# Turning the keys with VectorE in 32x32 blocks of 32-bit words, in a cached-attention decode kernel

## The chip, the cores and the metric

The kernel runs on one core of one Trainium2 chip. The metric is the time of the whole program in microseconds of device time, as a median of several runs. The traces are of one profiled execution each; a trace's span (first to last instruction) is about 2 us shorter than the run's time. In this kernel TensorE does the matrix products, VectorE and ScalarE the copies, reductions and exponentials, and GpSimd next to nothing (0.9 us busy before). HBM is the memory that the inputs are read from; the loads bring them to tiles in SBUF, and the profile takes their share over 16 DMA engines. The kernel keeps the products of TensorE in PSUM; to copy them from there to SBUF is to *evict* them. In the profiles PE is TensorE, PEld its loading of weights, DVE VectorE, ACT ScalarE and POOL GpSimd. The *granted clock* is the share of TensorE's full clock that it was given.

A single-core run shows no second die to compare with, so its "slow" label means only that the run is over 1.5% above the fastest run of the same kernel.

## The reference, cut to what matters

```python
# B=8 sequences, one new token each; Hq=16 query heads, Hkv=8 key/value heads, Dh=256, window W=1024
q = (x @ wq) -> [B, 16, 1, 256]
k, v = caches[:, :, Sk-W:, :]  (each head serves 2 query heads)
p = softmax(q @ k.T * Dh**-0.5);  a = (p @ v) @ wo
b = layernorm -> MLP(448 -> 1792 -> 448)
out = g * a + (1 - g) * b          # g: a sigmoid gate per token
```

The bytes are the keys and the values: 64 (sequence, head) pairs of 1024 x 256 bf16 each, keys and values 67 MB together, and 10.6 MB of weights. All are read once.

## The kernel before: the parts that matter

The work is cut into 16 *units* of four key/value heads. A unit has 2 MiB of keys (one tile in SBUF, partition = 32 positions x 4 heads) and 2 MiB of values. A ring of nine 2 MiB slots feeds everything: a load is issued as soon as a slot is released.

```python
RING = 9; LAG = 3                                # values of unit u are used LAG units later
def transpose_keys(u, between):                  # TensorE turns, ScalarE and VectorE evict
    for hf in range(2):
        for i in range(4):
            for c in range(8):
                nc.tensor.transpose(ktp[:, c, :], kn[:, o : o + P], ident[:])   # 128x128
            (nc.scalar.copy or nc.vector.tensor_copy)(kt[...], ktp[:])
            for step in between.get(g, ()): step()     # softmax of unit u-1 goes in between
    done()                                       # releases the slot of the keys

def scores(u):                                   # four heads side by side: 16 products of 628 ns in 2.01 us
    for hf in range(2):
        for j in range(2):
            for a in range(4):
                nc.tensor.matmul(S_ps[32*a : 32*a + 8, ...], lhsT=qw[:, j, b, half, a, :],
                                 rhs=KT[hf][:, j, :, a::4], ...)
...
for u in range(1, 16):
    transpose_keys(u, steps(u - 1))
    if u >= LAG: values(u - LAG)
    scores(u); top(u)
    if u >= LAG: finish(u - LAG)
```

## Time and profile before

| | before |
|---|---|
| time, median of 4 runs | 194.23 us (194.14 to 194.64) |
| span of the traced run | 192.3 us |
| HBM read | 77.68 MB |
| DMA, 50 to 170 us | share 1.01 of 16 engines, 425 GB/s |
| TensorE / VectorE / ScalarE busy | 78% / 63% / 44% |
| granted TensorE clock, mean | 0.910 |

The page of the profile. In the line of an engine, the figures are busy us, share of the span and number of instructions. The rows of digits are 40 slices of the span in tenths (9 is 90% or more). The last lines are groups of instructions: what was written and read, the count, then busy us and mean ns, then the idle time of that engine before them.

```profile
span 192.3 us, 4534 instructions
...
PE 150.7 (78%) x1990; PEld 104.7 (54%) x1990; DVE 121.5 (63%) x278; ACT 83.9 (44%) x102; POOL 0.9 (0%) x7
...
PEclk9998597899999999999999958999999999985558
DMA  5999999999999999999999999999999999999970
...
L342 ACT COPY kt<-ktp 128x1024 bf16<-128x1024 bf16 x64 | 63.2, 1017 | 70.8 <-PE ktp L339 70.8
L339 PE MATMUL ktp<-ident,slot 128*128 128x128 bf16 x1024 | 72.8, 229 | 19.3 <-ACT kt L342 10.4
...
L344 DVE COPY kt<-ktp 128x1024 bf16<-128x1024 bf16 x64 | 41.3, 684 | 15.0 <-PE ktp L339 15.0
L385 PE MATMUL S_ps<-kt,qw 128*8 128x512 bf16 x256 | 32.4, 628 | 0.3 <-DVE qw L375 0.3
```

The DMA row is full from the second slice to the last but two. What the change removes, the key transposes and their copies, is the largest work on three engines, but it runs under a full DMA. The chain of waits (start us, us, what), its end:

```profile
90.11 40.68 DMA slot<-in_A_k_cache_dram
130.85 39.20 DMA slot<-in_A_v_cache_dram
170.07 18.62 DMA slot<-in_A_wo_dram
```

From 90 us on the chain is nothing but loads. A unit's 4.19 MB take 9.8 to 9.9 us at 425 to 428 GB/s; that is the pace that any version must keep.

One more reading matters later: the granted clock of TensorE, by stretches (us; busy us of each engine; then clock, DMA share, GB/s).

```profile
50.00:170.00 120.00, 101.18 (x1306) 68.90 (x1304) 88.73 (x181) 62.79 (x78) 0.00 (x0) 0.97 1.01 425
...
109.50:110.50 1.00, 0.00 (x0) 0.00 (x0) 0.10 (x1) 0.00 (x0) 0.00 (x0) 0.70 1.07 442
110.50:111.50 1.00, 0.34 (x4) 0.35 (x5) 0.00 (x0) 0.00 (x0) 0.00 (x0) 0.50 1.00 426
```

TensorE is busy 84% of this time and its clock is 0.97 of full; once, while it waits for keys from 108.6 to 111.2 us, the clock falls to 0.50.

### The profile page before, as it was taken

The page shows a single profiled execution, that of the slowest core. Times are in us where ns is not written, and L with a number is a line of the kernel's source. Part 1 is how long each engine was busy: PE and PEld are TensorE (multiplying, and loading weights), DVE is VectorE, ACT ScalarE, POOL GpSimd, SP SyncE. Part 2 cuts the span into 40 slices and gives each one's busy share as a digit, 9 for nine tenths or more (in the row PEclk, how much of TensorE's full clock was granted, in tenths as well). Part 3 has the DMA queues.
Part 4 walks back from the last instruction along what each step waited for, and adds up shares of the span by engine and source line. Part 5 has one row for each costly group of instructions (what it writes and reads, how often), then busy time and mean ns, then how long its engine had stood idle before and what let it go on. Part 6 is the DMA issues. An engine that isn't in the chain of part 4 may idle for free.

```text
span 192.3 us, 4534 instructions
## 1 busy us (share of the span) xinstructions
PE 150.7 (78%) x1990; PEld 104.7 (54%) x1990; DVE 121.5 (63%) x278; ACT 83.9 (44%) x102; POOL 0.9 (0%) x7
## 2 busy tenths in 40 slices
PE   1199976999898988979888589896969697837672
PEld 0199624855756656575646286745554646413371
DVE  7632313767978787787958547776767676773310
ACT  2343020865848466382818154636354545520000
POOL 1000000000000000000000000000000000000000
PEclk9998597899999999999999958999999999985558
DMA  5999999999999999999999999999999999999970
GB/s 192 418 437 407 431 427 426 424 433 426 419 423 423 423 430 430 426 424 419 426 419 433 421 426 430 423 426 426 423 426 426 426 430 426 430 412 417 417 298 22
DMA packets 6742, 77.97 MB, mean 406 GB/s; under 512 B 946, under 2 KB 1347, under 8 KB 1987
## 3 DMA queue, kind: packets, MB, share of 16 engines
q1 hardware_dynamic: 6512, 77.67, 96.0%
q8 instruction: 15, 0.25, 0.5%
q10 hardware_dynamic: 210, 0.02, 0.1%
q14 instruction: 5, 0.03, 0.0%
HBM read 77.68 MB, written 0.01 MB: 404 GB/s over the span
## 4 chain that ended last, share of the span: by engine, by line
DMA 51%; PE 29%; ACT 12%; DVE 5%; issue 1%; ACTq 0%; DVEq 0%; SPq 0%
DMA slot<-in_A_k_cache_dram 21%; DMA slot<-in_A_v_cache_dram 20%; DMA slot<-in_A_wo_dram 10%; PE ktp L339 9%; PE S_ps L385 8%; ACT kt L342 7%; ACT E L405 4%; PE PO L446 3%; PE S_ps L356 2%; PE hT L494 2%; PE hT L484 1%; PE sm L471 1%; PE bb L532 1%; DVE nmx L397 1%; PE sm L424 1%
## 5 line engine op out<-in xcount | busy, mean ns | idle before, releaser
L342 ACT COPY kt<-ktp 128x1024 bf16<-128x1024 bf16 x64 | 63.2, 1017 | 70.8 <-PE ktp L339 70.8
L339 PE MATMUL ktp<-ident,slot 128*128 128x128 bf16 x1024 | 72.8, 229 | 19.3 <-ACT kt L342 10.4
L339 PEld LDWEIGHTS <-slot 128*128 128x128 bf16 x1024 | 67.1, 105 | 25.9 <-issue 15.5
L344 DVE COPY kt<-ktp 128x1024 bf16<-128x1024 bf16 x64 | 41.3, 684 | 15.0 <-PE ktp L339 15.0
L385 PE MATMUL S_ps<-kt,qw 128*8 128x512 bf16 x256 | 32.4, 628 | 0.3 <-DVE qw L375 0.3
L397 DVE TENSOR_REDUCE nmx<-S_ps 128x1 f32<-128x1024 f32 x16 | 19.6, 1225 | 15.0 <-PE S_ps L385 15.0
L413 DVE STREAM_TRANSPOSE EB<-E 128x1024 bf16<-128x1024 bf16 x16 | 19.9, 1245 | 7.0 <-ACT E L405 6.7
L405 ACT ACTIVATE E<-S_ps,nmx 128x1024 bf16<-128x1024 f32 x16 | 17.9, 1120 | 3.3 <-DVE nmx L398 3.3
L446 PE MATMUL PO<-slot,ET 128*16 128x512 bf16 x256 | 18.4, 410 | 1.2 <-DMA slot<-in_A_v_cache_dram 1.2
L385 PEld LDWEIGHTS <-qw 128*8 128x8 bf16 x256 | 7.3, 94 | 14.8 <-issue 10.4
L446 PEld LDWEIGHTS <-ET 128*16 128x16 bf16 x256 | 5.4, 91 | 6.8 <-issue 2.2
L426 DVE CAST ET<-sm 128x256 bf16<-128x256 f32 x16 | 6.6, 414 | 0.7 <-PE sm L424 0.7
L474 DVE CAST oT<-sm 128x16 bf16<-128x16 f32 x16 | 3.5, 220 | 3.3 <-PE sm L471 3.3
L424 PE MATMUL sm<-selr,ones_f 128*128 128x8 f32 x32 | 5.3, 239 | 0.0
L424 PEld LDWEIGHTS sm<-selr,ones_f 128*128 128x128 f32 x32 | 5.0, 196 | 0.5 <-issue 0.4
L421 PE MATMUL sm<-EB,perm 128*128 128x256 bf16 x16 | 4.5, 279 | 0.3 <-DVE oT L474 0.3
L594 PE MATMUL A_ps<-slot,oP 128*8 128x112 bf16 x128 | 3.8, 287 | 0.8 <-DMA slot<-in_A_wo_dram 0.8
L504 DVE TENSOR_TENSOR z<-hT,b_sb 128x112 f32<-128x112 f32 x1 | 0.3, 275 | 5.5 <-PE hT L494 5.5
L594 PEld LDWEIGHTS <-oP 128*8 128x8 bf16 x128 | 2.9, 116 | 1.6 <-issue 1.6
L356 PE MATMUL S_ps<-slot,xT 128*8 128x512 bf16 x32 | 3.4, 607 | 0.0
L229 PE MATMUL tp<-ident,y_sb 8*128 8x8 bf16 x3 | 0.2, 170 | 3.8 <-DVE y_sb L280 3.8
L405 ACT ACTIVATION_READ_ACCUMULATOR E<-S_ps,nmx 128x1 f32 x16 | 3.2, 202 | 0.0
(143 smaller groups left out, 86.8 us busy)
## 6 DMA issues: line engine op xcount, KB each, us to landing
slot<-in_A_v_cache_dram SPq DMA_DIRECT2D x16, 2048.0 KB, 37.5
slot<-in_A_k_cache_dram SPq DMA_DIRECT2D x15, 2048.0 KB, 34.5
slot<-in_A_wo_dram SPq DMA_DIRECT2D x3, 896.0 KB, 31.0
slot<-in_A_k_cache_dram SPq DMA_DIRECT2D x2, 1024.0 KB, 7.1
slot<-in_A_wq_dram SPq DMA_DIRECT2D x1, 2048.0 KB
slot<-in_B_w_dram SPq DMA_DIRECT2D x1, 1568.0 KB
slot<-in_B_w_dram SPq DMA_DIRECT2D x1, 1344.0 KB, 9.7
slot<-in_A_wq_dram SPq DMA_DIRECT2D x1, 1024.0 KB
```

The costliest lines, as they stand in the source:

```text
L339: nc.tensor.transpose(ktp[:, c, :], kn[:, o : o + P], ident[:])
L342: nc.scalar.copy(dst, ktp[:])
L344: nc.vector.tensor_copy(dst, ktp[:])
L356: nc.tensor.matmul(S_ps[32 * t : 32 * t + NB, n * QN : (n + 1) * QN], lhsT=xT[:, r + half, :], rhs=w[:, o + c : o + c + QN], start=(r == 0 ...
L385: nc.tensor.matmul(S_ps[32 * a : 32 * a + RQ, hf * CH * SK : (hf + 1) * CH * SK], lhsT=qw[:, j, b, half, a, :], rhs=KT[hf][:, j, :, a::QUA ...
L397: nc.vector.reduce_max(nmx[:], S_ps[:], axis=AXIS.X, negate=True)
L405: nc.scalar.activation(E[:], S_ps[:], ACT.Exp, bias=nmx[:], scale=1.0, accum_out=rowsum[:])
L413: nc.vector.transpose(EB[:].rearrange("p c r -> p (c r)"), E[:])
L424: nc.tensor.matmul(sm[:, NCK, :], lhsT=ones_f[:], rhs=selr[:], start=True, stop=True)
L426: nc.vector.tensor_copy(ET[:], sm[:, 0:NCK, :])
L446: nc.tensor.matmul(PO[32 * t : 32 * t + PAIR * RQ], lhsT=ET[:, PAIR * c : PAIR * (c + 1), :], rhs=vn[:, PAIR * c * Dh : PAIR * (c + 1) * D ...
L594: nc.tensor.matmul(dst, lhsT=oP[:, j, q, :], rhs=w[:, o + cols.start : o + cols.stop], start=(q == 0 and j == 0), stop=(q == NHQ - 1 and j ...
```

## The change

The intent: take the 1024 key transposes from TensorE and their 128 evictions from ScalarE and VectorE. VectorE instead turns 32x32 blocks of 32-bit words straight from SBUF to SBUF (two bf16 go as one word). This leaves the keys of the four heads mixed in blocks on the partitions, so the scores use *block-diagonal* queries: full-width products of 128 columns, eight per half unit, plus one that puts a large negative number where the head is foreign. The maximum of a row group is then shared among blocks by a small fp32 product (`share`). LAG goes from 3 to 2, and scores get two PSUM buffers.

```diff
-    LAG = 3
+    LAG = 2
...
-                        nc.tensor.transpose(ktp[:, c, :], kn[:, o : o + P], ident[:])
-                    dst = kt[:, j, c0 : c0 + NC, :]
-                    if g in (0, 3, 4, 7):
-                        nc.scalar.copy(dst, ktp[:])
-                    else:
-                        nc.vector.tensor_copy(dst, ktp[:])
+        nc.vector.transpose(
+            KT[u, hf][:, c0 : c0 + PIECE].rearrange("p c k x r -> p (c k x r)").bitcast(WORD),
+            kn[:, o : o + PIECE * Dh].bitcast(WORD),
+        )
...
+        nc.tensor.matmul(S[u][:, cols], lhsT=foreign[:], rhs=place[:], start=True, stop=False)
+        for k in range(NK):                      # 4
+            for par in range(NPAR):              # 2
+                nc.tensor.matmul(S[u][:, cols], lhsT=qw[:, j, u, m * RQ : m * RQ + P],
+                                 rhs=kt[:, :, k, :, par], start=False, stop=...)
...
+    def share(u):
+        nc.tensor.matmul(mz[:], lhsT=same[:], rhs=m4[:], start=True, stop=True)
+        nc.vector.reduce_max(nmx[:], mz[:], axis=AXIS.X, negate=True)
+        nc.scalar.activation(E, S, ACT.Exp, bias=nmx[:], ...)
...
     for u in range(1, NQ):
-        transpose_keys(u, steps(u - 1))
-        if u >= LAG:
-            values(u - LAG)
-        scores(u)
-        top(u)
+        for piece in range(CH // PIECE):
+            turn_keys(u, 0, piece)
+        scores(u, 0)
+        top(u - 1)
+        turn_keys(u, 1, 0)
+        share(u - 1)
+        turn_keys(u, 1, 1)
+        if u >= LAG:
+            values(u - LAG)
+        scores(u, 1)
+        turn(u - 1)
+        if u >= LAG:
+            gather(u - LAG)
+        invert(u - 1)
         if u >= LAG:
             finish(u - LAG)
```

More of the change, by code (lines that the diff above doesn't have):

```diff
@@ L13 @@
 F32 = mybir.dt.float32
+WORD = mybir.dt.int32
 PSUM = bass.MemoryType.PSUM
@@ L64 @@
     CH = NCK // NH
+    NU = NQ
     SLOT = 8192
@@ L70 @@
     RING = 9
-    LAG = 3
+    LAG = 2
+    NK = 4
+    NPAR = 2
+    KP = NK * NPAR
+    BLK = 32
+    PIECE = 8
     BIG = 1e30
@@ L80 @@
     ring = ctx.enter_context(tc.tile_pool(name="ring", bufs=RING))
-    ktpool = ctx.enter_context(tc.tile_pool(name="ktpool", bufs=4))
+    ktpool = ctx.enter_context(tc.tile_pool(name="ktpool", bufs=3))
     epool = ctx.enter_context(tc.tile_pool(name="epool", bufs=2))
     opool = ctx.enter_context(tc.tile_pool(name="opool", bufs=LAG + 1))
-    ps_s = ctx.enter_context(tc.tile_pool(name="ps_s", bufs=1, space=PSUM))
-    ps_kt = ctx.enter_context(tc.tile_pool(name="ps_kt", bufs=3, space=PSUM))
-    ps_sm = ctx.enter_context(tc.tile_pool(name="ps_sm", bufs=1, space=PSUM))
+    ps_s = ctx.enter_context(tc.tile_pool(name="ps_s", bufs=2, space=PSUM))
+    ps_sm = ctx.enter_context(tc.tile_pool(name="ps_sm", bufs=2, space=PSUM))
     ps_po = ctx.enter_context(tc.tile_pool(name="ps_po", bufs=1, space=PSUM))
@@ L191 @@
     nc.gpsimd.memset(ones_f[:], 1.0)
-    S_ps = ps_s.tile([P, W], F32)
-    nc.vector.memset(S_ps[:], 0.0)
+    Sq = ps_s.tile([P, W], F32, tag="S", name="Sq")
+    nc.vector.memset(Sq[:], 0.0)
     PO = ps_po.tile([P, PAIR, Dh], F32)
@@ L214 @@
     own = consts.tile([P, PAIR], F32)
-    qw = consts.tile([P, NJ, NB, Hq // RQ, QUAD, RQ], BF16)
+    AREA = P + BLK
+    qw = consts.tile([P, NJ, NU, AREA], BF16)
+    pick = consts.tile([P, NK // NJ, NPAR, P], BF16)
+    same = consts.tile([P, P], F32)
+    block = consts.tile([P, QUAD], F32)
+    foreign = consts.tile([P, P], BF16)
+    place = consts.tile([P, CH, BLK], BF16)
     oT = consts.tile([P, Hq, NJ, NB], BF16)
@@ L236 @@
     transposed(xT, x_sb, xz)
+    by_col = ident[:].rearrange("p (b r) -> p b r", b=QUAD)
+    by_row = ident[:].rearrange("p (b r) -> p r b", b=QUAD)
+    nc.vector.reduce_sum(sel[:], by_row[:, 0:RQ, :], axis=AXIS.X)
+    nc.vector.reduce_sum(block[:], by_col, axis=AXIS.X)
+    zrow = consts.tile([P, BLK], F32)
+    nc.vector.reduce_sum(zrow[:], by_row, axis=AXIS.X)
+    nc.vector.tensor_copy(
+        same[:].rearrange("p (b r) -> p b r", b=QUAD),
+        zrow[:].rearrange("p (o r) -> p o r", o=1).to_broadcast([P, QUAD, BLK]),
+    )
@@ L237 @@
+    pairs = zrow[:, 0 : PAIR * RQ].rearrange("p (q i) -> p q i", i=PAIR)
+    nc.vector.reduce_sum(sel2[:], pairs, axis=AXIS.X)
+    nc.vector.reduce_sum(own[:], pairs.rearrange("p q i -> p i q"), axis=AXIS.X)
+    head = consts.tile([BLK, QUAD], F32)
     nc.vector.reduce_sum(
-        sel[:], ident[:].rearrange("p (a s) -> p s a", a=QUAD)[:, 0:RQ, :], axis=AXIS.X
-    )
-    halfs = ident[:].rearrange("p (a s) -> p s a", a=QUAD)
-    for i in range(PAIR):
-        nc.vector.reduce_sum(
-            own[:, i : i + 1], halfs[:, i * RQ : (i + 1) * RQ, :], axis=AXIS.XY
-        )
@@ L245 @@
-    nc.vector.reduce_sum(
-        sel2[:],
-        ident[:]
-        .rearrange("p (a h s) -> p s a h", a=QUAD, s=RQ)[:, :, :, 0:PAIR],
-        axis=AXIS.XY,
-    )
-    perm = consts.tile([P, P], BF16)
-    nc.vector.tensor_copy(
-        perm[:].rearrange("p (s a) -> p s a", a=QUAD),
-        ident[:].rearrange("p (a s) -> p s a", a=QUAD),
-    )
-    cap = consts.tile([P, 1], F32)
-    rows = consts.tile([P, 1], F32)
-    for a in range(QUAD):
-        nc.vector.reduce_sum(
-            rows[32 * a : 32 * a + 32, :],
-            ident[32 * a : 32 * a + 32, (32 + rep) * a : (32 + rep) * a + rep],
-            axis=AXIS.X,
-        )
@@ L264 @@
-    nc.vector.tensor_scalar(
-        cap[:], rows[:], 2.0 * BIG, -BIG, op0=ALU.mult, op1=ALU.add
-    )
+        head[:],
+        ident[0:BLK, 0:BLK].rearrange("p (s a) -> p a s", a=QUAD),
+        axis=AXIS.X,
+    )
+    nc.vector.tensor_scalar(
+        head[:], head[:], BIG, -BIG, op0=ALU.mult, op1=ALU.add
+    )
+    nc.vector.memset(foreign[:], 0.0)
+    for i in range(rep):
+        nc.vector.tensor_copy(
+            foreign[0:BLK, :].rearrange("p (b r) -> p b r", b=QUAD)[:, :, i:RQ:rep],
+            head[:].rearrange("p (o a) -> p o a", o=1).to_broadcast([BLK, QUAD, QUAD]),
+        )
@@ new lines @@
+    nc.vector.tensor_copy(
+        place[:],
+        ident[:, 0:BLK].rearrange("p (o x) -> p o x", o=1).to_broadcast([P, CH, BLK]),
+    )
+    for kk in range(NK // NJ):
+        for par in range(NPAR):
+            nc.vector.tensor_copy(
+                pick[:, kk, par, :].rearrange("p (b w) -> p b w", b=QUAD),
+                ident[:]
+                .rearrange("p (k o w r) -> p k r o w", k=NK // NJ, o=1, r=NPAR)[:, kk, par]
+                .to_broadcast([P, QUAD, BLK]),
+            )
@@ L326, with turn_keys @@
     KT = {}
-    def transpose_keys(u, between=None):
+    def turn_keys(u, hf, piece):
         kn = slot("k", u)
-        between = between or {}
-        for hf in range(NH):
-            kt = ktpool.tile([P, NJ, CH, P], BF16, tag="kt", name="kt")
-            KT[hf] = kt
-            for i in range(CH // NC * NJ):
-                    c0, j = i // NJ * NC, i % NJ
-                    g = hf * (CH // NC * NJ) + i
-                    ktp = ps_kt.tile([P, NC, P], BF16, tag="ktp", name="ktp")
-                    for c in range(NC):
-                        o = (hf * CH + c0 + c) * Dh + j * P
-                        nc.tensor.transpose(ktp[:, c, :], kn[:, o : o + P], ident[:])
-                    dst = kt[:, j, c0 : c0 + NC, :]
-                    if g in (0, 3, 4, 7):
-                        nc.scalar.copy(dst, ktp[:])
-                    else:
-                        nc.vector.tensor_copy(dst, ktp[:])
-                    for step in between.get(g, ()):
-                        step()
-        done()
+        if piece == 0:
+            KT[u, hf] = ktpool.tile(
+                [P, CH, NK, BLK, NPAR], BF16, tag="kt", name="kt"
+            )
+        c0 = piece * PIECE
+        o = (hf * CH + c0) * Dh
+        nc.vector.transpose(
+            KT[u, hf][:, c0 : c0 + PIECE]
+            .rearrange("p c k x r -> p (c k x r)")
+            .bitcast(WORD),
+            kn[:, o : o + PIECE * Dh].bitcast(WORD),
+        )
+        if (hf + 1) * CH == NCK and c0 + PIECE == CH:
+            done()
     def query():
@@ L356, in query @@
                     nc.tensor.matmul(
-                        S_ps[32 * t : 32 * t + NB, n * QN : (n + 1) * QN],
+                        Sq[32 * t : 32 * t + NB, n * QN : (n + 1) * QN],
                         lhsT=xT[:, r + half, :],
@@ L364, in query @@
         done(2)
-        qs = consts.tile([P, W], BF16)
-        nc.scalar.activation(qs[:], S_ps[:], ACT.Copy, scale=qscale)
-        qt = ps_kt.tile([P, NC, P], BF16, tag="ktp", name="qt")
-        for m in range(NC):
-            nc.tensor.transpose(qt[:, m, :], qs[:, m * P : (m + 1) * P], ident[:])
-        qv = qt[:].rearrange(
-            "p (c i j) (g d s) -> p d c j s g i", c=2, i=rep, j=NJ, g=Hq // RQ, d=2
-        )
-        for a in range(QUAD):
-            for j in range(NJ):
-                nc.vector.tensor_copy(
-                    qw[:, j, :, :, a, a * rep : (a + 1) * rep],
-                    qv[:, a // 2, a % 2, j, 0:NB],
-                )
@@ L380, in scores @@
-    def scores(u):
-        b, half = divmod(u, Hkv // QUAD)
-        for hf in range(NH):
-            for j in range(NJ):
-                for a in range(QUAD):
-                    nc.tensor.matmul(
-                        S_ps[32 * a : 32 * a + RQ, hf * CH * SK : (hf + 1) * CH * SK],
-                        lhsT=qw[:, j, b, half, a, :],
-                        rhs=KT[hf][:, j, :, a::QUAD],
-                        start=(j == 0),
-                        stop=(j == NJ - 1),
-                    )
+        qs = epool.tile([P, W], BF16, tag="E", name="qs")
@@ new lines, in query @@
+        nc.scalar.activation(qs[:], Sq[:], ACT.Copy, scale=qscale)
+        qt = ps_sm.tile([P, HPQ, NJ, P], BF16, tag="sm", name="qt")
+        for hh in range(HPQ):
+            for j in range(NJ):
+                o = (hh * NJ + j) * P
+                nc.tensor.transpose(qt[:, hh, j, :], qs[:, o : o + P], ident[:])
+        qd = consts.tile([P, NJ, NB, 2, 2, HPQ], BF16)
+        for j in range(NJ):
+            for half in range(2):
+                nc.vector.tensor_copy(
+                    qd[:, j, :, half],
+                    qt[:, :, j, 64 * half : 64 * half + 64]
+                    .rearrange("p h (q b) -> p b q h", q=2)[:, 0:NB],
+                )
@@ new lines, in query @@
+        qp = ps_s.tile([P, NJ, NU, QUAD, RQ], F32, tag="S", name="qp")
+        for j in range(NJ):
+            for kk in range(NK // NJ):
+                for par in range(NPAR):
+                    nc.tensor.matmul(
+                        qp[:, j, :, kk * NPAR + par, :],
+                        lhsT=pick[:, kk, par, :],
+                        rhs=qd[:, j].rearrange("p b h q i -> p (b h) (q i)"),
+                        start=True,
+                        stop=True,
+                    )
@@ new lines, in query, with scores @@
+        for b in range(QUAD):
+            rows = slice(BLK * b, BLK * (b + 1))
+            dst = qw[rows, :, :, BLK * b : BLK * (b + 1)]
+            src = qp[rows].rearrange("p j u m q -> p j u (m q)")
+            if b % 2 == 0:
+                nc.scalar.copy(dst, src)
+            else:
+                nc.vector.tensor_copy(dst, src)
+    S = {}
+    def scores(u, hf):
+        if hf == 0:
+            S[u] = ps_s.tile([P, W], F32, tag="S", name="S")
+        cols = slice(hf * CH * BLK, (hf + 1) * CH * BLK)
+        kt = KT.pop((u, hf))
+        nc.tensor.matmul(
+            S[u][:, cols], lhsT=foreign[:], rhs=place[:], start=True, stop=False
+        )
+        for k in range(NK):
+            for par in range(NPAR):
+                j, m = k // (NK // NJ), k % (NK // NJ) * NPAR + par
+                nc.tensor.matmul(
+                    S[u][:, cols],
+                    lhsT=qw[:, j, u, m * RQ : m * RQ + P],
+                    rhs=kt[:, :, k, :, par],
+                    start=False,
+                    stop=(k == NK - 1 and par == NPAR - 1),
+                )
@@ L393 @@
     soft = {}
     def top(u):
-        nmx = epool.tile([P, 1], F32, tag="nmx", name="nmx")
-        nc.vector.reduce_max(nmx[:], S_ps[:], axis=AXIS.X, negate=True)
-        nc.vector.tensor_tensor(nmx[:], nmx[:], cap[:], op=ALU.min)
-        soft[u] = nmx
-    def expo(u):
-        nmx = soft.pop(u)
-        E = epool.tile([P, W], BF16, tag="E", name="E")
+        mx = epool.tile([P, 1], F32, tag="mx", name="mx")
+        nc.vector.reduce_max(mx[:], S[u][:], axis=AXIS.X)
+        m4 = epool.tile([P, QUAD], F32, tag="m4", name="m4")
@@ L404, in expo @@
+        nc.vector.tensor_scalar_mul(m4[:], block[:], mx[:])
+        soft[u] = m4
+    def share(u):
+        m4 = soft.pop(u)
+        mz = ps_sm.tile([P, QUAD], F32, tag="sm", name="mz")
+        nc.tensor.matmul(mz[:], lhsT=same[:], rhs=m4[:], start=True, stop=True)
+        nmx = epool.tile([P, 1], F32, tag="nmx", name="nmx")
+        nc.vector.reduce_max(nmx[:], mz[:], axis=AXIS.X, negate=True)
+        E = epool.tile([P, NCK // PAIR, BLK, PAIR], BF16, tag="E", name="E")
         rowsum = epool.tile([P, 1], F32, tag="rowsum", name="rowsum")
@@ L405, in expo @@
         nc.scalar.activation(
-            E[:], S_ps[:], ACT.Exp, bias=nmx[:], scale=1.0, accum_out=rowsum[:]
+            E[:].rearrange("p c x i -> p c i x"),
+            S.pop(u)[:].rearrange("p (c i x) -> p c i x", i=PAIR, x=BLK),
+            ACT.Exp,
+            bias=nmx[:],
+            scale=1.0,
+            accum_out=rowsum[:],
         )
@@ L411, in turn, with invert @@
         E, rowsum = soft.pop(u)
-        EB = epool.tile([P, NCK, 32], BF16, tag="EB", name="EB")
-        nc.vector.transpose(EB[:].rearrange("p c r -> p (c r)"), E[:])
+        ET = opool.tile([P, NCK // PAIR, BLK, PAIR], BF16, tag="ET", name="ET")
+        nc.vector.transpose(
+            ET[:].rearrange("p c r i -> p (c r i)").bitcast(WORD),
+            E[:].rearrange("p c x i -> p (c x i)").bitcast(WORD),
+        )
         selr = epool.tile([P, RQ], F32, tag="selr", name="selr")
         nc.vector.tensor_scalar_mul(selr[:], sel[:], rowsum[:])
-        soft[u] = (EB, selr)
-    def bring(u):
-        EB, selr = soft.pop(u)
-        sm = ps_sm.tile([P, NCK + 1, RQ], F32, tag="sm", name="sm")
-        nc.tensor.matmul(
-            sm[:, 0:NCK, :], lhsT=perm[:], rhs=EB[:, :, 0:RQ], start=True, stop=True
-        )
-        nc.tensor.matmul(sm[:, NCK, :], lhsT=ones_f[:], rhs=selr[:], start=True, stop=True)
-        ET = opool.tile([P, NCK, RQ], BF16, tag="ET", name="ET")
-        nc.vector.tensor_copy(ET[:], sm[:, 0:NCK, :])
+        sm = ps_sm.tile([P, RQ], F32, tag="sm", name="sm")
+        nc.tensor.matmul(sm[:], lhsT=ones_f[:], rhs=selr[:], start=True, stop=True)
+        soft[u] = (ET, sm)
+    def invert(u):
+        ET, sm = soft.pop(u)
         rb = epool.tile([P, RQ], F32, tag="rb", name="rb")
-        nc.vector.reciprocal(rb[:], sm[:, NCK, :])
+        nc.vector.reciprocal(rb[:], sm[:])
         rsel = opool.tile([P, RQ], F32, tag="rsel", name="rsel")
@@ L431, in bring @@
         soft[u] = (ET, rsel)
-    def steps(u):
-        return {
-            0: [lambda: expo(u)],
-            2: [lambda: turn(u)],
-            6: [lambda: bring(u)],
-        }
     def values(u):
@@ L447, in values @@
                 PO[32 * t : 32 * t + PAIR * RQ],
-                lhsT=ET[:, PAIR * c : PAIR * (c + 1), :],
+                lhsT=ET[:, c, 0:RQ, :],
                 rhs=vn[:, PAIR * c * Dh : PAIR * (c + 1) * Dh],
@@ L453, in values, with gather @@
         done()
+        soft[u] = rsel
+    def gather(u):
+        rsel = soft.pop(u)
         os_ = epool.tile([P, Dh], F32, tag="os", name="os_")
@@ L546 @@
     norm_and_gate()
-    transpose_keys(0)
+    for hf in range(NH):
+        for piece in range(CH // PIECE):
+            turn_keys(0, hf, piece)
     hs = mlp_hidden()
     query()
-    scores(0)
-    top(0)
+    for hf in range(NH):
+        scores(0, hf)
     mlp_out(hs)
     for u in range(1, NQ):
-        transpose_keys(u, steps(u - 1))
+        for piece in range(CH // PIECE):
+            turn_keys(u, 0, piece)
[4 more added lines that the diff above has]
+        turn_keys(u, 1, 1)
         if u >= LAG:
             values(u - LAG)
-        scores(u)
-        top(u)
+        scores(u, 1)
[3 more added lines that the diff above has]
+        invert(u - 1)
         if u >= LAG:
@@ L561 @@
     u = NQ - 1
-    expo(u)
+    top(u)
+    share(u)
     turn(u)
-    values(u - 2)
-    finish(u - 2)
-    bring(u)
     values(u - 1)
+    gather(u - 1)
+    invert(u)
     A_ps = ps_misc.tile([P, DO], F32, tag="misc", name="A_ps")
@@ L574, in spread_rows @@
     def spread_rows(q0, q1):
-        pp = ps_kt.tile([P, HPQ, NJ, q1 - q0, NB], F32, tag="ktp", name="pp")
+        pp = ps_sm.tile([P, HPQ, NJ, q1 - q0, NB], F32, tag="sm", name="pp")
         for i in range(HPQ):
@@ L604 @@
     values(u)
+    gather(u)
     finish(u)
```

## The prediction

> **What bounds it now: the DMA stream.** The 40 slices show DMA over 90% busy almost throughout; the table by stretches gives 424 to 426 GB/s at a DMA share of 1.00 from 50 to 170 us. The HBM line says 77.68 MB, so about 183 us of pure transfer. One unit (four heads; 2 MiB of keys, 2 MiB of values) needs 4.19 MB / 0.4255 = 9.86 us. TensorE (78% busy), VectorE (63%) and ScalarE (44%) fit underneath; in the timeline key transposes wait for DMA (1.2 to 2.6 us). The chain of waits is DMA from 90 to 188.7 us. So nothing taken off an engine pays over about 1%.
>
> **What the change does, per unit.**
> - Removed: 64 TensorE transposes (72.8 us busy, 4.5 us a unit), their eight evictions (ScalarE 1017 ns, VectorE 684 ns), the perm product and its 414 ns copy.
> - Added to VectorE: four 32-bit transposes of 1024 words. The existing 1024-element transpose took 1245 ns; I assume the same per word, 1.17 us start to start: 4.7 us a unit. The softmax transpose halves.
> - Scores: 16 matmuls ran four side by side in 2.0 us; now 18 full-width ones run in sequence. From value groups of four (0.25 us) I estimate 0.22 us each at full clock, 0.43 at half (as query groups).
> - The 4-byte stride should be harmless[...]. No trace shows it yet.
>
> **Critical path.** VectorE's own sum is about 8.4 us of the 9.86. But engines wait on each other in program order: turn, turn (2.3) -> reduce_max, small multiply (1.4) -> turn (1.2) -> shared maximum from TensorE -> turn (1.2) while exp runs (1.1) -> softmax transpose, gather (1.9) -> wait for nine score matmuls and the sum -> reciprocal, rsel -> wait for the fp32 finish product (0.64) -> copy -> next keys. Adding durations: about 10.0 us a unit at full clock, above the DMA's 9.86.
>
> And the clock will not stay full. TensorE idles about 2.6 us a unit while the first two turns run. In the trace before, such a gap (108.6 to 111.2 us) dropped the granted clock to 0.50 until 116.7, and another at 171.35; the changes are multiples of 3.41 us apart[...]. If each gap drops the clock, half the scores run at 0.43 us and a unit takes 11 to 12 us.
>
> Setup: 4 us more VectorE constants; unit 1 starts near 34 to 38 us (32.9 before). LAG 2 makes the last keys land 4.9 us later, exposing the tail after the last scores (about 22 us).
>
> Sum: 36 + 9.5 + 13 x 11.2 + 10 + 22.5 = 224 us. At full clock 203; at 12 us a unit 235.
>
> **Prediction: 224 us, 80% range 196 to 242. Faster 0.03, same 0.18, slower 0.79.**
>
> **What would show it.** DMA share below 0.9 mid-run; chain of waits on VectorE turns and score matmuls; granted clock mean 0.6 to 0.85 between 50 and 170 us; key transposes about 1245 ns x64 (80 us); score spacing 0.22/0.43 us; unit spacing 11 to 12 us.
>
> **What would make it wrong.** A clock that stays full: 196 to 203. Unit below 9.5 us: DMA-bound, 192 to 197. 32-bit transposes at half rate, or strided keys slowing the matmuls: over 242.

The 3.41 us stand by the trace of before: its clock changes at 109.91, 116.74 and 171.35 us, 2 x 3.41 and 16 x 3.41 us apart.

## The result, and the profile after

| | before | after |
|---|---|---|
| time, median of 4 runs | 194.23 us (194.14 to 194.64) | 212.32 us (210.46 to 215.31) |
| ratio of fast runs | | 1.0896 (1.0841 to 1.0951) |
| span of the traced run | 192.3 us | 210.8 us |
| DMA, 50 to 170 us | 1.01, 425 GB/s | 1.01, 428 GB/s |
| TensorE / VectorE / ScalarE busy | 78% / 63% / 44% | 66% / 70% / 14% |
| granted clock, 50 to 170 us | 0.97 | 0.84 |
| last piece of DMA on the chain | ends 188.7 us | none on the chain |

A ratio is the mean time of one kernel's fast runs over that of the other's in the same rounds, so it is not quite the ratio of the medians. One of the four runs after (215.31) is slow and is not in the ratio.

The page after:

```profile
span 210.8 us, 2528 instructions
...
PE 140.1 (66%) x1013; PEld 70.6 (34%) x1022; DVE 148.1 (70%) x282; ACT 29.7 (14%) x40; POOL 0.8 (0%) x7
...
PEclk9999999858888789978888887879797969696555
DMA  5999999999999999999999999999999999910000
...
L431 PE MATMUL S<-kt,qw 128*128 128x512 bf16 x256 | 81.9, 476 | 44.2 <-DVE kt L358 39.2
L358 DVE STREAM_TRANSPOSE kt<-slot 128x1024 int32<-128x1024 int32 x64 | 77.1, 1226 | 0.0
...
L456 ACT ACTIVATE E<-S,nmx 128x1024 bf16<-128x1024 f32 x16 | 22.6, 1412 | 140.1 <-DVE nmx L453 140.1
```

Two things are to be seen. The DMA row is as full as before, and then it is empty for the last eighth: all loads have landed at about 185 us (the stretch from 180 to 187 us still has 298 GB/s), earlier than before, and the engines need another 26 us. And VectorE's key transposes have "0.0" idle before them: the keys lay ready each time. So the loss is a backlog of the engines, which the nine slots of the ring hide from the DMA row until the loads are over.

One unit in the timeline of after (start us, us, engine, line, operation, operands; in brackets the idle time before it and what ended that):

```profile
99.11 1.19 DVE L443 TENSOR_REDUCE mx<-S 128x1 f32<-128x1024 f32 x1
99.23 3.36 PE L431 MATMUL S<-kt,qw 128*128 128x512 bf16 x8 [2.31 <-DVE kt L358]
...
102.43 0.28 PE L451 MATMUL mz<-m,same 128*128 128x4 f32 x2
...
102.75 0.16 DVE L453 TENSOR_REDUCE nmx<-mz 128x1 f32<-128x4 f32 x1 [1.04 <-PE mz L451]
...
104.11 1.90 PE L431 MATMUL S<-kt,qw 128*128 128x512 bf16 x8 [0.43 <-DVE kt L358]
...
106.28 0.64 PE L522 MATMUL sm<-rsel,os__926 128*128 128x8 f32 x4
106.42 0.17 DVE L484 TENSOR_TENSOR rsel<-rb,sel 128x8 f32<-128x8 f32 x1
106.77 0.38 PE L425 MATMUL S<-place,foreign 128*128 128x512 bf16 x1
106.95 0.23 DVE L525 CAST oT<-sm 128x16 bf16<-128x16 f32 x1 [0.37 <-PE sm L522]
```

The same eight score matmuls take 3.36 us in the first half of the unit and 1.90 us in the second. The next unit's `nmx` is at 112.98 us, so a unit takes 10.23 us. The stretches of the same trace, cut at the changes of the clock:

```profile
50.00:170.00 120.00, 88.32 (x498) 41.32 (x504) 98.79 (x169) 17.53 (x24) 0.00 (x0) 0.84 1.01 428
...
95.50:98.90 3.40, 1.28 (x9) 0.89 (x8) 2.98 (x6) 0.00 (x0) 0.00 (x0) 0.99 0.99 419
98.90:102.30 3.40, 3.06 (x8) 1.10 (x8) 2.77 (x4) 0.00 (x0) 0.00 (x0) 0.51 1.03 439
102.30:105.70 3.40, 2.96 (x28) 1.44 (x28) 2.52 (x5) 1.45 (x2) 0.00 (x0) 1.00 1.00 424
105.70:109.10 3.40, 1.31 (x9) 0.91 (x8) 2.96 (x6) 0.00 (x0) 0.00 (x0) 0.99 1.01 424
```

In a stretch of 3.4 us TensorE is busy only 1.3 us (38%), because VectorE is turning keys. At its end the clock falls to 0.5. After one stretch that is 90% busy it returns to 1.00, and so round. A unit is three such stretches. From 51.05 to 190.99 us every change of the clock in this trace lies on a grid of 3.413 us (41 steps), and each fall up to there lasts one step (98.84 to 102.25 us, for one); I call a step of this grid a *window*. 3 x 3.413 = 10.24 us, and the trace has units of 10.23.

### The profile page after: what moved, and what is told of

The parts are those of the page before. It is cut to its first block, busy times and chain, and to the rows that moved or that the text cites. A ratio compares the mean times of both kernels' runs of the same rounds, so it can differ in the third digit from the quotient of the medians.

```text
span 210.8 us, 2528 instructions
## 1 busy us (share of the span) xinstructions
PE 140.1 (66%) x1013; PEld 70.6 (34%) x1022; DVE 148.1 (70%) x282; ACT 29.7 (14%) x40; POOL 0.8 (0%) x7
## 4 chain that ended last, share of the span: by engine, by line
PE 46%; DVE 38%; ACT 10%; issue 3%; ACTq 0%
PE S L431 27%; DVE kt L358 17%; ACT E L456 8%; PE sm L522 5%; DVE ET L469 4%; PE PO L493 3%; DVE oT L525 2%; PE Sq L374 2%; PE A_ps L656 1%; PE hT L545 1%; PE hT L535 1%; PE mz L451 1%; DVE qw L416 1%; DVE nmx L453 1%; DVE mx L443 1%
## 5 line engine op out<-in xcount | busy, mean ns | idle before, releaser
L431 PE MATMUL S<-kt,qw 128*128 128x512 bf16 x256 | 81.9, 476 | 44.2 <-DVE kt L358 39.2
L358 DVE STREAM_TRANSPOSE kt<-slot 128x1024 int32<-128x1024 int32 x64 | 77.1, 1226 | 0.0
L431 PEld LDWEIGHTS <-qw 128*128 128x128 bf16 x256 | 28.7, 112 | 86.8 <-issue 67.8
L456 ACT ACTIVATE E<-S,nmx 128x1024 bf16<-128x1024 f32 x16 | 22.6, 1412 | 140.1 <-DVE nmx L453 140.1
L443 DVE TENSOR_REDUCE mx<-S 128x1 f32<-128x1024 f32 x16 | 19.0, 1187 | 0.0
L469 DVE STREAM_TRANSPOSE ET<-E 128x512 int32<-128x512 int32 x16 | 11.4, 711 | 8.0 <-ACT E L456 8.0
L451 PEld LDWEIGHTS mz<-m,same 128*128 128x128 f32 x32 | 7.4, 235 | 6.6 <-issue 3.9
L425 PE MATMUL S<-place,foreign 128*128 128x512 bf16 x23 | 9.2, 400 | 0.0
L425 PEld LDWEIGHTS <-foreign 128*128 128x128 bf16 x32 | 4.8, 149 | 7.0 <-issue 6.9
L451 PE MATMUL mz<-m,same 128*128 128x4 f32 x32 | 5.1, 230 | 1.7 <-DVE m L445 1.7
```

The costliest lines, as they stand in the source:

```text
L358: nc.vector.transpose(KT[u, hf][:, c0 : c0 + PIECE] .rearrange("p c k x r -> p (c k x r)") .bitcast(WORD), kn[:, o : o + PIECE * Dh].bitca ...
L425: nc.tensor.matmul(S[u][:, cols], lhsT=foreign[:], rhs=place[:], start=True, stop=False)
L431: nc.tensor.matmul(S[u][:, cols], lhsT=qw[:, j, u, m * RQ : m * RQ + P], rhs=kt[:, :, k, :, par], start=False, stop=(k == NK - 1 and par = ...
L443: nc.vector.reduce_max(mx[:], S[u][:], axis=AXIS.X)
L451: nc.tensor.matmul(mz[:], lhsT=same[:], rhs=m4[:], start=True, stop=True)
L456: nc.scalar.activation(E[:].rearrange("p c x i -> p c i x"), S.pop(u)[:].rearrange("p (c i x) -> p c i x", i=PAIR, x=BLK), ACT.Exp, bias=n ...
```

## The experiments

Theory A: the fall of the clock in each unit puts the unit above the DMA's pace of 9.8 us. Rival B: the hand-offs between VectorE and TensorE in program order do it, whatever the clock. Rival C: the longer start and the tail are the loss. A last theory, of a lock: the unit is held at three windows of 3.41 us. All runs below were correct. "Before" ran beside each of them and stayed at 194.13 to 194.32 us in the median.

### e1_warm: TensorE is kept busy with useless work

```diff
+    def keep_warm(n):
+        for _ in range(n):
+            nc.tensor.matmul(warm[:], lhsT=ident[:], rhs=place[:]..., start=True, stop=True)
...
         if u >= LAG:
             finish(u - LAG)
+        keep_warm(8)
```

> Edit: eight useless 512-column matmuls per unit on TensorE, after the finish product, into an unused PSUM bank, so that it does not idle while VectorE turns the next keys. They add work only. Theory A (the halved clock in the first score group of each unit is what puts the unit over the DMA's pace): the first eight score matmuls of a unit take about 1.9 us in place of 3.4, the wait of the maximum (nmx) for TensorE goes from 1.0 us to under 0.2, the unit from 10.24 to about 9.1 us, the run to about 198 us (196 to 202). Rival B (the hand-offs between VectorE and TensorE in program order set the unit, whatever the clock): unit stays at 10.0 us or more, the run at 208 to 214. Rival C (the start and the tail are the loss): unit may shrink but the run stays above 206.

Measured: 196.2 us (195.09 to 197.58), ratio to before 1.0112 (1.0062 to 1.0162). The timeline of e1_warm:

```profile
123.08 0.12 DVE L453 TENSOR_REDUCE nmx<-mz 128x1 f32<-128x4 f32 x1
...
124.77 0.71 DVE L469 STREAM_TRANSPOSE ET<-E 128x512 int32<-128x512 int32 x1 [0.41 <-ACT E L456]
...
126.46 0.21 DVE L482 RECIPROCAL rb<-sm 128x8 f32<-128x8 f32 x1
...
127.23 0.23 DVE L525 CAST oT<-sm 128x16 bf16<-128x16 f32 x1 [0.36 <-PE sm L522]
...
127.26 1.67 PE L610 MATMUL warm<-place,ident 128*128 128x512 bf16 x7
128.77 0.38 PE L425 MATMUL S<-place,foreign 128*128 128x512 bf16 x1
129.73 1.90 PE L431 MATMUL S<-kt,qw 128*128 128x512 bf16 x8 [0.58 <-DVE kt L358]
...
132.12 0.12 DVE L453 TENSOR_REDUCE nmx<-mz 128x1 f32<-128x4 f32 x1
```

The useless matmuls are those of `warm`. The score group takes 1.90 us, `nmx` no longer waits, the unit takes 9.04 us, and the clock is 1.00 from 50 to 170 us. Added work made the program about 16 us shorter. The order of the instructions is that of after, so rival B's claim that a unit needs 10 us whatever the clock falls, and C falls as the main cause. What is left to before (1.1%) was not taken apart; in e1's tail, which is on the chain of waits, the clock is 0.50 again (180 to 185 us). The lines of VectorE show its only two waits in this unit, 0.41 us for the exponential and 0.36 us for the finish product.

### e2_ahead: the next keys are turned before the waits

```diff
+    ahead(1)                                   # turn_keys(1, 0, *)
     for u in range(1, NQ):
-        for piece in range(CH // PIECE):
-            turn_keys(u, 0, piece)
         scores(u, 0)
...
             gather(u - LAG)
+        if u + 1 < NQ:
+            ahead(u + 1)
         invert(u - 1)
```

> Edit: VectorE turns the first half of the next unit's keys right after the gather, ahead of the reciprocal and of the copy that waits for the finish product; no work added or removed. The gap of TensorE should shrink from 2.3 us to about 1.2 us. Theory A (clock): with so short a gap the clock mostly holds, the unit takes 8.9 to 9.7 us, the run 198 to 206 us. If the clock still falls every unit, the unit is locked to three 3.41 us windows and stays at 10.24 us, run about 212. Rival B (hand-offs): removing about 1 us of waits from VectorE's order gives about 9.2 us a unit even if the clock still shows 0.5 in the first score group.

Measured: 197.18 us (196.66 to 197.51), ratio 1.0157 (1.0138 to 1.0175). The shared maxima in its timeline:

```profile
113.15 0.12 DVE L453 TENSOR_REDUCE nmx<-mz 128x1 f32<-128x4 f32 x1
122.46 0.16 DVE L453 TENSOR_REDUCE nmx<-mz 128x1 f32<-128x4 f32 x1 [0.70 <-PE mz L451]
131.06 0.12 DVE L453 TENSOR_REDUCE nmx<-mz 128x1 f32<-128x4 f32 x1
```

The run is a little below the range of theory A. A unit with a full clock takes 8.60 us here, the one shown in which it fell 9.31; over 14 units (42.44 to 168.82 us) the mean is 9.03, with three waits for keys (1.7 us) from 139.6 us on, where the engines have caught up with the loads. The gap of TensorE is 1.4 us and the clock still falls in about every second unit (mean 0.87 to 0.91 between 50 and 170 us). What each repair is worth depends on the other:

| us a unit | the clock falls | the clock is full |
|---|---|---|
| order of after | 10.24 (after) | 9.04 (e1) |
| order of e2 | 9.24 (five units of e2 before 139.6 us, 8.96 to 9.47) | 8.60 (e2) |

The order is worth 1.0 us a unit where the clock falls and 0.4 where it is full; the clock is worth 1.2 in the old order and 0.6 in the new. With the clock fallen the new order gives the 9.2 us of rival B, so e2 alone does not decide between A and B. Either repair alone brings the unit below the DMA's 9.8 us (for the order this is read from single units; in no run with it did the clock fall in all of them). A and B are not exclusive: the order makes the gap, and the gap costs the clock. I had put the locked case at 10.24 us; it did not come.

### e3_pad and e9_warm_pad: is the unit locked to the windows?

```diff
         if u >= LAG:
             finish(u - LAG)
+        nc.vector.memset(idle[:], 0.0)         # 128x256; e9_warm_pad also has keep_warm(8)
```

> Edit: one more VectorE memset (128x256, about 0.2 us from start to start) in each unit, between the copy of the finish product and the next turns, on the chain as traced. Plain chain: every unit 0.2 us longer, 10.44 us, the run 2.6 us longer. Theory of a lock (the clock falls and rises on a fixed grid of 3.41 us, and a score group that starts later in its window has more matmuls at full clock): the spacing of the units stays at 10.24 us = 3 x 3.413, the run unchanged within 1 us of a run with the same phase.

Measured: 215.21 us (214.23 to 216.54), ratio 1.1092 (1.104 to 1.1145). The maxima of e3_pad:

```profile
104.09 0.16 DVE L453 TENSOR_REDUCE nmx<-mz 128x1 f32<-128x4 f32 x1 [1.36 <-PE mz L451]
113.87 0.12 DVE L453 TENSOR_REDUCE nmx<-mz 128x1 f32<-128x4 f32 x1
124.61 0.16 DVE L453 TENSOR_REDUCE nmx<-mz 128x1 f32<-128x4 f32 x1 [1.36 <-PE mz L451]
```

Units now alternate between about 9.8 us (clock full) and 10.7 us (clock halved through the values as well). Two together take 20.5 us, six windows. From 104.09 to 165.60 us the mean is 10.25 us, against 10.24 in after (102.75 to 164.17 us): the memset was absorbed. But the run as a whole was 2.9 us longer, which is what the plain chain foretold and not the lock; in after the units between 53.7 and 82.4 us, not yet settled, took 9.4 to 9.8 us, and in e3_pad those of that time already took 10.3 to 10.8. So this run supports the lock for the steady part and misses on the total. Hence a control at full clock:

> Edit: e1's eight useless matmuls a unit and e3's extra VectorE memset (0.19 us from start to start in e3's trace) together. Control for the lock. In e3, with the clock falling, the memset moved the mean spacing of the units from 10.24 to 10.26 us only. If the grid of clock windows is what absorbed it, then with the clock held at 1.00 there is nothing to absorb it, and every unit takes 9.05 + 0.19 = 9.24 us, all equal. If the memset was simply hidden in a wait of VectorE, the units stay at 9.05 us here too.

Measured: 199.43 us (two runs, 198.96 and 199.90). Its maxima:

```profile
106.93 0.12 DVE L453 TENSOR_REDUCE nmx<-mz 128x1 f32<-128x4 f32 x1
116.23 0.12 DVE L453 TENSOR_REDUCE nmx<-mz 128x1 f32<-128x4 f32 x1
125.52 0.12 DVE L453 TENSOR_REDUCE nmx<-mz 128x1 f32<-128x4 f32 x1
```

Every unit takes 9.30 us: the memset costs 0.25 us each time at full clock, 0.06 more than I had read from its spacing. With the clock falling, it cost 0.01. e4_start and e6_lag3 below settle at 10.23 to 10.25 us too. This agrees with a lock. One part of it can be read in after: a first score group that begins 0.44 us into a half-clock window (89.04 us) takes 3.33 us, one that begins 0.37 us into one (119.69 us) 3.37. Why the round trip should end at a whole number of windows was not shown.

### e4_start: the start alone

```diff
-    nc.vector.memset(qw[:], 0.0)
+    nc.gpsimd.memset(qw[:], 0.0)
...
+    for piece in range(CH // PIECE):
+        turn_keys(1, 0, piece)
     mlp_out(hs)                                # and not again in the loop for u = 1
```

> Edit: only the start. The zeroing of the query tile (2.2 us on VectorE) goes to GpSimd, and VectorE turns the first half of unit 1's keys while TensorE computes unit 0's scores, before the MLP's output copy. Rival C (the start is a large part of the loss): run 4 us or more shorter. Theory A: the loop starts 2 to 3 us earlier and the units keep 10.2 us, so the run is 2 to 3 us shorter (about 209 to 210) and not more.

Measured: 206.55 us (205.48 to 209.51), ratio 1.0623 (1.0567 to 1.068): 5.8 us below the median of after (5.3 us by the ratios). That is a miss for my 2 to 3 us and meets what C expected (4 us or more): the start is worth more than I allowed, though e1, with the old start, shows that it is not the main cause. The first shared maximum came only 2.25 us earlier (40.23 us against 42.48), and the units settle at 10.24 us as foretold. The profile fell on the slowest of the four runs (209.51, slow), so the other 3 us can't be placed in a trace. Kernels whose clock falls in nearly every unit spread by 1.7 to 4.9 us from run to run (e6, e3_pad, e4_start, after) and e7 below by 0.3 us; but e1, whose clock stays full, spreads by 2.5 us too. The cause of the spread was not shown.

### e6_lag3: is LAG 2 to blame?

```diff
-    LAG = 2
+    LAG = 3                                    # and one more values step in the tail
```

(Two temporaries of the MLP share a buffer, to make room.)

> Edit: LAG 3 in the changed kernel, with a tail for one more values step, as in the kernel before (two temporaries of the MLP share a buffer to make room). Nothing else. It tests the step of the prediction that blames LAG 2 for keys that land late. If the last keys' landing is not waited for (VectorE's key transposes show no idle in the trace of after), nothing is gained: 211 to 216 us. If LAG 2 is a cause, 3 to 5 us shorter: 207 to 209.

Measured: 213.59 us (212.77 to 214.44), ratio 1.1001 (1.097 to 1.1032): nothing gained. Keys that land 4.9 us earlier (an estimate: one load of 2.1 MB at 428 GB/s) only lie there longer.

### e5_all, e7_all_lag3, e8_tail: the repairs together

e5 joins the three repairs (four useless matmuls a unit); e7 is e5 with LAG 3; e8 is e7 with 20 useless matmuls in the tail.

```diff
# e5: keep_warm(4) at the end of a unit; ahead(u + 1) after gather; ahead(1) before mlp_out; qw zeroed on GpSimd
# e7: e5 and
-    LAG = 2
+    LAG = 3
# e8: e7 and, in the last units' softmax,
+    keep_warm(8)      # before share(u)
+    keep_warm(8)      # after values(u - 2)
+    keep_warm(4)      # after finish(u - 2)
```

> Edit: the three repairs of e1, e2 and e4 together (four useless matmuls a unit in place of eight, the next keys turned ahead, the shorter start). By addition: units of 8.6 us (as e2's warm units), the loop about 2.5 us earlier than e1's, so the engines catch up with the DMA (9.8 us a unit) before the end and the last keys' landing (about 161.5 us by the bytes behind it at 428 GB/s) sets the rest: about 192.5 us (191.5 to 194), 0.5 to 1% below the kernel before. If the repairs do not add (rival: something else holds e1 and e2 near 196), it stays at 195 to 197.

> Edit: e5 with LAG 3. Here the engines keep up, so the landing of the last keys should matter: they land 4.9 us earlier (one value load more behind them). Expected 190 to 191.5 us, 1 to 2 us below e5, held by the end of the DMA (about 185 us) plus 4 us of projection and output. If the landing of the last keys does not matter in e5 either, equal to e5 or 1 us longer.

> Edit: e7 with useless matmuls also in the tail (20 in the softmax and gather waits of the last units), to keep the clock at full there: the traced tails run at 0.5. If the tail after the last scores is on the critical path in e7, 1 to 3 us shorter than e7; if the DMA's end is, equal within 0.5 us.

| | us | ratio to before |
|---|---|---|
| e5_all | 195.41 (195.24 to 196.37) | 1.0072 (1.0052 to 1.0091) |
| e7_all_lag3 | 192.76 (192.6 to 192.86) | 0.9923 (0.991 to 0.9935) |
| e8_tail | 192.82 (192.61 to 193.13) | 0.9927 (0.9914 to 0.994) |

In e5 the units take 8.54 us until about 91 us, then the engines have caught up and each unit takes 9.8 us, the DMA's pace. I had expected 192.5 us (191.5 to 194); 195.41 lies where I had put the rival, that the repairs do not add. Within the units they do add (8.54 us); what holds the run is its end. VectorE began to turn the last unit's keys at 163.4 us, after a wait for their load, 2 us later than my sum of bytes said, and the tail behind them took from about 172.7 us (last scores) to 194.3, at clock 0.50 from 180 us on. There LAG 3 pays: e7 is 2.65 us shorter than e5, where e6 was no shorter than after. It still missed its 190 to 191.5 us: I had put the end of the DMA at about 185 us. The end of the chain of waits of e7:

```profile
91.36 38.00 DMA slot<-in_A_k_cache_dram
129.42 39.16 DMA slot<-in_A_v_cache_dram
168.60 18.68 DMA slot<-in_A_wo_dram
```

This is the picture of before again: loads from 91 us to 187.3 us. e8 is equal to e7 within 0.1 us (clock 1.00 against 0.61 from 170 to 180 us, 0.82 against 0.50 from 180 to 185, then 0.50 against 0.84), so the tail's clock costs nothing here, where the loads end last. e7 beats both kernels, by 0.8% (clear of the noise, but "same" by the rule of 2%) and 9%. Why its last load ends 1.4 us earlier than before's (187.3 against 188.7 us) was not tested.

## Why the prediction was right or wrong

The prediction said slower, 224 us with 196 to 242; 212.32 was measured. Point by point:

- **"Nothing taken off an engine pays over about 1%": right.** The best version found gains 0.8%, with the DMA at its end.
- **The clock: right, and the larger of two causes.** A mean of 0.6 to 0.85 was foretold, 0.84 was measured; e1 shows what it costs, 10.24 - 9.04 = 1.2 us a unit. The other is the order of the hand-offs, which makes the gap (e2). The prediction had "slower" at full clock too (203 us); there it would have been wrong by e1, so "slower" came out right only because the clock fell.
- **"About 10.0 us a unit at full clock, above the DMA's 9.86": wrong.** e1 has 9.04 us at clock 1.00, below the DMA's pace. The step that failed is in the chain of the critical path: "wait for nine score matmuls and the sum -> reciprocal, rsel -> wait for the fp32 finish product (0.64)". The other terms of the chain leave about 0.7 us of the 10.0 for this first wait and the one for the shared maximum (an estimate from the prediction's terms and the durations in after). In e1 neither is there: the reciprocal at 126.46 us and `nmx` at 132.12 us follow with no wait. For the finish product VectorE waits 0.36 us, not 0.64, since that product uses the `rsel` of an earlier unit: in the timeline of after it starts at 106.28 us, before this unit's `rsel` at 106.42. Also, the opening product of each score group (L425) needs no keys and runs ahead, so eight matmuls and not nine stand behind the turned keys. What each of these gives of the 1 us was not tested one by one. Without the clock, the change would have been about 1% slower than before (e1), not 4.5% ("At full clock 203").
- **"If each gap drops the clock ... a unit takes 11 to 12 us": the clock's part right, the base too large.** The mean from unit 2 to unit 14 was 10.05 us. For the clock 11.2 - 10.0 = 1.2 us had been added, and 1.2 us was measured; half of the scores run at half clock, as foretold (3.36 us against 1.90). So the error is that of the base above, 10.0 for 9.04. In the sum this term was 13 x 11.2 = 146; it measured 130.7, 15 us less. The others together were 2 us too small: start 36 (37.3 measured), unit 1 9.5 (10.7), last unit 10 (9.2), tail 22.5 (22.9). 37.3 + 10.7 + 130.7 + 9.2 + 22.9 = 210.8, the span.
- **"DMA share below 0.9": wrong.** It was 1.01. I took the DMA to stall when the engines fall behind; with nine slots it did not before it was done. The backlog shows at the end, as a tail with an empty DMA row.
- **"LAG 2 ... exposing the tail": wrong for this kernel.** The tail is exposed because the engines come late, not because the keys do (e6). It becomes true once they keep up (e5 against e7).
- **The costs on VectorE: right.** Key transposes took 1226 ns (1245 assumed, the time of 128x1024 bf16 elements in before: here a word took as long as an element of half its bytes), 77.1 us in all (80), VectorE was busy 98.79 of 120 us, or 8.4 us per 10.24 us unit (8.4). Missed: the exponential on ScalarE took 1412 ns in place of 1120 (its output is now written with a step of two elements; that this is the reason was not tested); it ends after the last turn, and VectorE waits 0.43 us for it.
- **"The 4-byte stride should be harmless": right.** Eight matmuls take 1.90 us at full clock with it; seven of `warm` in e1, which read without a step, take 1.67, the same for each (0.24 us).

## What to carry to other kernels

When work leaves TensorE, look at the gap that it leaves: here a 2.3 us wait for VectorE in every settled unit halved the clock for the next 3.4 us, and in e2 gaps of 1.4 us did in about every second unit (three of the six from 91 to 139 us). The gap is not all: in the settled units of after a window with 1.3 busy us of 3.4 lost the clock, and 3.0 of 3.4 kept it or brought it back. In between, the busy time of the trace draws no line: 2.07 us of 3.41 lost it in before (106.5 to 109.91 us), 1.71 us of 3.40 kept it in after (78.3 to 81.7 us). Useless matmuls that only keep TensorE busy made the program 16 us shorter, and an order with a shorter gap 15 us. A full DMA row does not prove that the engines keep up (after had a share of 1.01 and a tail of 26 us): with a deep ring look at whether the consumers ever wait for a load, and at how long the tail behind the last load is. Undo a suspected cause both in the broken version and in the repaired one: LAG cost nothing in the first and 2.65 us in the second.
